# Attention turned on its side: keys on the partitions, no row maximum, strided heads in blocks of seven classes, gate logits computed transposed, and a flag that guards a second, shifted version

## The chip, the cores and the metric

The kernel runs on one core of one Trainium2 chip. The metric is the device time of one execution in microseconds (us), lower is better. The time before is the median of 8 executions. A profiled execution gives the trace that is read below; it is one more execution with its own time.

## What is computed

The program is attention followed by a mixture of experts with one expert per token. There are 8 batches (b), 8 heads of 64, and 576 positions. Heads 0 to 3 are *local*: position s sees keys s-31 to s. Heads 4 to 7 are *strided*: position s sees the earlier keys whose position has the same remainder modulo 32. Cut to what matters:

```python
scores = q @ k.T / 8
scores = where(mask_local or mask_strided, scores, -1e9)
scores = scores - max(scores)                  # per query row
attn = exp(scores); attn = attn / (sum(attn) + 1e-9)
x = attn @ v                                   # (8, 576, 512) after joining the heads
logits, local_gate = x @ w_gate, sigmoid(x @ w_local)
e = argmax(logits) if s == 0 or local_gate < 0.5 else the previous token's e
out = softmax(logits)[e] * (relu(x @ w1[e]) @ w2[e])   # w1: 512x1024, w2: 1024x512, 8 experts
```

Everything is float32.

## The kernel before, in words

Three stages follow one another.

**Attention** (`attention`, L82 to L309) works through 64 units in the order batch, pair of heads, half: `Unit(b, pair, g)`. Pairs 0 and 1 are local, 2 and 3 strided. Queries lie on the partitions. A local unit has three blocks of 96 queries against 128 keys, for two heads; a strided unit has four blocks of 72 queries against 72 keys. One unit goes through:

- `scores`: per head one matmul that writes the mask into PSUM (L175, bf16), then one matmul per block on top of it (L180, `sps`). The two heads of a pair sit on partitions 0 to 63 and 64 to 127. VectorE takes the row maximum (L184) and subtracts it (L187), ScalarE does the exponential (L189).
- `turn`: the exponentials are transposed block by block on TensorE (L197, `tps`), and ScalarE copies them to SBUF (L200).
- `values`: one matmul per block against v with a column of ones appended (L210). VectorE adds 1e-9 to the row sum, takes its reciprocal, and scales (L219 to L221).
- After a second pair, `store_x` writes 96 or 72 rows at a time to the DRAM tensor `xd` through SyncE's queue; `turn_x` transposes x into `xT` (L241, with ScalarE's copies L245 and L247).
- Once per batch `gates` computes the logits: 24 float32 matmuls with 96 columns of `xT` as the stationary operand and nine columns of the gate weights moving (L255).

A float32 matmul shows as two records in the profile, a transpose and a bf16 matmul as one. The order is that of a software pipeline (L284 to L309): step n does the scores of unit n, the transposes of n-1, the values of n-2, `turn_x` and `gates` of n-3; a planner may move instructions within it. Loads of the next batch's group are issued on SyncE when a group begins. During batch 1 the weights of expert 0 are loaded and GpSimd forms sums of their quarters (`Weights.ready`, L507 and L512).

**Routing** (`route`, L312 to L485) turns the gate results into tables of rows for each expert: small VectorE steps in a chain and the matmuls L475. A part for experts with over 6 tiles of 128 rows and their remainder is skipped by a branch unless it is needed.

**Experts** (`experts`, L526 on) gathers rows from `xd` with indirect DMAs, multiplies with a two-by-two scheme of seven products (L608 and L644, and L684 and L692 for a single tile), and scatters the result. The list after the last expert (the rows that didn't fit) is skipped by a branch on `count`.

Of the kernel before, what the change touches and what calls it, by code (L numbers as in the profile page):

```python
# [8 lines left out]
F32 = mybir.dt.float32  # L9
# [9 lines left out]
P = 128  # L19
# [17 lines left out]

QP = 3
XT = 2 * QP + 1
NT = E * XT  # L40
OT = 2 * (N // (2 * P) - QP)
# [30 lines left out]
@with_exitstack  # L72
def attention_then_scomoe(ctx: ExitStack, tc: tile.TileContext, q, k, vl, vs, wg, w1, w2, out):
    nc = tc.nc
    once = ctx.enter_context(tc.tile_pool(name="once", bufs=1))
    dram = ctx.enter_context(tc.tile_pool(name="dram", bufs=1, space=DRAM))
    xd = dram.tile([N, D], F32, name="xd")

    ident = once.tile([P, P], F32, name="ident")
    make_identity(nc, ident)  # L80
    gi = once.tile([P, NT + OT], I32, name="gi")
    si = once.tile([P, NT + OT], I32, name="si")  # L82
    gate = once.tile([P, NT + OT], F32, name="gate")
    pick = once.tile([1, E], I32, name="pick")
    oet = once.tile([1, OT], I32, name="oet")
    on = once.tile([1, 1], I32, name="on")
    tabs = gi, si, gate, pick, oet, on
    one = Weights(once)

    with ExitStack() as first:  # L90
        routing = first.enter_context(tc.tile_pool(name="routing", bufs=1))
        probs = routing.tile([LQ, LT, B, E], F32, name="probs")
        codes = routing.tile([LQ, LT, B, E], F32, name="codes")
        with ExitStack() as part:
            attention(part, tc, q, k, vl, vs, wg, xd, ident, probs, codes, lambda: one.ready(nc, w1, w2, 0))
        with ExitStack() as part:
            route(part, tc, ident, probs, codes, tabs)
    with ExitStack() as part:
        with tc.manual_schedule():
            experts(part, tc, xd, w1, w2, out, ident, tabs, one)  # L100


def attention(ctx, tc, q, k, vl, vs, wg, xd, ident, probs, codes, weights):
# [183 lines left out]
    for n in range(len(units) + 3):  # L287
        if n < len(units):
            u = units[n]
            if u.g == 0 and u.pair % 2 == 0:  # L290
                b, grp = u.b + 1, u.pair // 2
                if b < B:
                    load(b, grp)
                if b == 2 and grp == 1:
                    weights()
            scores(u)
# [15 lines left out]
def route(ctx, tc, ident, probs, codes, tabs):  # L312

    nc = tc.nc
    gi, si, gate, pick, oet, on = tabs
# [63 lines left out]
    nn = rp.tile([R, 2], F32, name="nn")  # L379
    nc.vector.tensor_copy(nn, nps[:, 0:2])  # L380
    qi = rp.tile([R, 1], I32, name="qi")
    nc.vector.tensor_scalar(qi, nn[:, 0:1], float(P - 1), None, Alu.add)
    nc.vector.tensor_scalar(qi, qi, 8, None, Alu.arith_shift_right)
    qf = rp.tile([R, 1], F32, name="qf")
    nc.vector.tensor_scalar(qf, qi, 1, None, Alu.max)
    ov = rp.tile([R, 1], F32, name="ov")
    nc.vector.tensor_scalar(ov, qf, -float(QP), 0.0, Alu.add, Alu.max)
    nc.tensor.matmul(nps[:, 2:3], lhsT=less[0:E, :], rhs=ov[0:E], start=True, stop=True)
    nc.tensor.matmul(nps[0:1, 3:4], lhsT=ones[0:E, 0:1], rhs=ov[0:E], start=True, stop=True)
    q2 = rp.tile([R, 1], F32, name="q2")  # L390
    nc.vector.tensor_scalar(q2, qf, float(2 * P), None, Alu.mult)
    pk = rp.tile([R, 1], F32, name="pk")
    nc.vector.tensor_scalar(pk, qf, float(QP), 2.0, Alu.min, Alu.mult)
    nc.vector.tensor_scalar(pk, pk, -2.0, None, Alu.add)
    nc.vector.scalar_tensor_tensor(pk, nn[:, 0:1], q2, pk, Alu.is_gt, Alu.add)
    pps = pp.tile([1, E + OT], F32, name="pps")
    nc.tensor.matmul(pps[:, 0:E], lhsT=pk[0:E], rhs=ident[0:E, 0:E], start=True, stop=True)
    nc.vector.tensor_copy(pick, pps[:, 0:E])
    nc.vector.tensor_copy(on, nps[0:1, 3:4])
    obase = rp.tile([R, 1], F32, name="obase")  # L400
    nc.vector.tensor_copy(obase, nps[:, 2:3])
    oend = rp.tile([E, 1], F32, name="oend")
    nc.vector.tensor_tensor(oend, obase[0:E], ov[0:E], op=Alu.add)
    past = rp.tile([E, OT], F32, name="past")
    nc.vector.tensor_scalar(past, io[0:E, 0:OT], 0.5, None, Alu.mult)
    pasti = rp.tile([E, OT], I32, name="pasti")
    nc.vector.tensor_scalar(past, past, -0.25, None, Alu.add)
    nc.vector.tensor_copy(pasti, past)
    nc.vector.tensor_copy(past, pasti)
    nc.vector.tensor_scalar(past, past, oend, None, Alu.is_ge)  # L410
    nc.tensor.matmul(pps[:, E:], lhsT=ones[0:E, 0:1], rhs=past, start=True, stop=True)
    nc.vector.tensor_scalar(oet, pps[:, E:], float(E - 1), None, Alu.min)

    first = rp.tile([R, 1], F32, name="first")
    nc.vector.tensor_scalar(first, er, float(XT * P), None, Alu.mult)

    far = rp.tile([R, 1], F32, name="far")
    nc.vector.tensor_scalar(far, obase, float(2 * P), float((E * XT - 2 * QP) * P), Alu.mult, Alu.add)
    nc.vector.tensor_tensor(far, far, first, op=Alu.subtract)
    isov = rp.tile([R, 1], F32, name="isov")  # L420
    nc.vector.tensor_scalar(isov, ov, 0.0, None, Alu.is_gt)
    nc.vector.tensor_tensor(far, far, isov, op=Alu.mult)
    rest = rp.tile([R, 1], F32, name="rest")
    nc.vector.tensor_scalar(rest, q2, -1.0, float(2 * QP * P), Alu.mult, Alu.add)
    nc.vector.tensor_tensor(rest, rest, far, op=Alu.subtract)
    rank0 = rp.tile([R, 1], F32, name="rank0")
    nc.vector.tensor_scalar(rank0, nn[:, 1:2], -1.0, None, Alu.add)
    rank = rp.tile([R, S], F32, name="rank")
    nc.vector.tensor_scalar(rank, cum, rank0, None, Alu.add)
    sa = rp.tile([R, S], F32, name="sa")  # L430
    nc.vector.tensor_scalar(sa, rank, float(2 * QP * P), far, Alu.is_ge, Alu.mult)
    sb = rp.tile([R, S], F32, name="sb")
    nc.vector.tensor_scalar(sb, rank, q2, rest, Alu.is_ge, Alu.mult)
    nc.vector.scalar_tensor_tensor(rank, rank, first, sa, Alu.add, Alu.add)
    nc.vector.tensor_tensor(rank, rank, sb, op=Alu.add)
    slot = rp.tile([R, S], F32, name="slot")
    nc.vector.tensor_tensor(slot, rank, hot, op=Alu.mult)
# [17 lines left out]

    lane = rp.tile([LQ, CM, P], F32, name="lane")
    for a, n in ((0, NT), (NT, OT)):
        if a:
            more = tc.If(nc.values_load(on[0:1, 0:1], engines=[ET.PE, ET.DVE, ET.Activation, ET.Pool], min_val=0,
                                        max_val=OT // 2,  # L460
                                        skip_runtime_bounds_check_because="a count of at most 15 pairs") > 0)
            more.__enter__()
        put = rp.tile([LQ, CM, 2, n], F32, name=f"put{a}")
        at = rp.tile([LQ, CM, n], F32, name=f"at{a}")
        nc.vector.tensor_tensor(at, across(io[0:LQ, a:a + n], [LQ, CM, n]), spread(hi, [LQ, CM, n]), op=Alu.is_equal)
        nc.gpsimd.tensor_tensor(put[:, :, 0], at, spread(tok, [LQ, CM, n]), op=Alu.mult)
        nc.vector.tensor_tensor(put[:, :, 1], at, spread(pt, [LQ, CM, n]), op=Alu.mult)
        tab = pp.tile([P, 2, n], F32, name=f"tab{a}")
        for t in range(LT):
            c = slice(t * B, (t + 1) * B)  # L470
            if not a:
                nc.vector.tensor_tensor(lane[:, c], across(io[0:LQ], [LQ, B, P]), spread(lo[:, c], [LQ, B, P]),
                                        op=Alu.is_equal)
            for i in range(t * B, (t + 1) * B):
                nc.tensor.matmul(tab, lhsT=lane[:, i], rhs=put[:, i], start=(i == 0), stop=(i == CM - 1))  # L475
        nc.scalar.copy(out=gate[:, a:a + n], in_=tab[:, 1])
        row = rp.tile([P, n], F32, name=f"rowf{a}")
        nc.vector.tensor_scalar(row, tab[:, 0], -1.0, 0.0, Alu.add, Alu.max)
        nc.vector.tensor_copy(gi[:, a:a + n], row)
        skip = rp.tile([P, n], F32, name=f"skip{a}")  # L480
        nc.vector.tensor_scalar(skip, tab[:, 0], 0.0, float(SKIP), Alu.is_equal, Alu.mult)
        nc.vector.tensor_tensor(row, row, skip, op=Alu.add)
        nc.vector.tensor_copy(si[:, a:a + n], row)
        if a:
            more.__exit__(None, None, None)  # L485
# [315 lines left out]
```

## Time and profile before

| | us |
|---|---|
| median of 8 executions (lowest, highest) | 1054.32 (1029.85, 1064.69) |
| the profiled execution | 1041.75 |
| its span, first to last instruction | 1040.0 |
| attention: first score matmul L180 to the last gate step on VectorE | 6.42 to 414.67 |
| routing: first matmul L358 to the first transpose of the experts L569 | 414.69 to 476.88 |
| experts: L569 to the end of the last scatter's issue | 476.88 to 1025.61 |
| busy over the span: TensorE matmul, weight load | 959.6, 863.3 |
| busy over the span: VectorE, ScalarE, GpSimd | 428.1, 240.2, 249.7 |

The parts of such a page: busy time of each engine, then the span in 40 slices (26 us each) with the clock granted to TensorE, then the DMA queues, then the chain of work that ended last, then the costliest groups. Groups are named by line, engine, operation and tile (`out<-in`), with the number of instructions, the busy time, and the mean duration of one. Matmuls overlap in the pipeline, so a price per matmul is read from start to start in the timeline, not from a mean duration.

### The profile page before, as it was taken

The numbers are of one execution on the slowest core, as the hardware profiler recorded it, in microseconds if no ns is written. First come the engines' busy times: TensorE is split into PE (matmuls) and PEld (weight loads), VectorE is DVE, ScalarE is ACT, GpSimd is POOL, SyncE is SP. The second block draws the span as 40 slices with busy tenths as digits, with TensorE's granted clock in tenths as the row PEclk, the third lists the DMA queues.
The fourth block names the chain that finished last, engine by engine and source line by source line (L and its number), as shares of the span: only waits on it lengthen the run. The fifth ranks groups of instructions, "written<-read, shape, count | busy, mean of one in ns | idle before, by whom it ended". The sixth has DMA issues, their size and how long they took to land.

```text
span 1040.0 us, 16153 instructions
## 1 busy us (share of the span) xinstructions
PE 959.6 (92%) x6632; PEld 863.3 (83%) x6632; DVE 428.1 (41%) x870; ACT 240.2 (23%) x389; POOL 249.7 (24%) x227
## 2 busy tenths in 40 slices
PE   7999999999999998286999898999999999899993
PEld 6888888888888888276998797979989989798893
DVE  6643434343444433831333535325333343532431
ACT  3422222222232321001222122222222222222220
POOL 1330000000000000204332625348173272533000
PEclk9855555555555555557999999999999999999997
DMA  9651414132322001006006043060520515201000
GB/s 320 231 201 50 144 47 135 59 109 86 101 93 67 27 5 42 1 1 244 22 21 209 34 149 105 21 214 22 190 77 21 197 43 177 76 21 41 29 21 19
DMA packets 35523, 95.54 MB, mean 92 GB/s; under 512 B 3278, under 2 KB 12494, under 8 KB 34768
## 3 DMA queue, kind: packets, MB, share of 16 engines
q1 hardware_dynamic: 28416, 73.58, 20.6%
q0 software_dynamic: 6400, 19.93, 5.7%
q8 instruction: 67, 1.10, 0.4%
q14 instruction: 112, 0.92, 0.3%
q10 hardware_dynamic: 528, 0.02, 0.0%
HBM read 74.64 MB, written 19.92 MB: 91 GB/s over the span
## 4 chain that ended last, share of the span: by engine, by line
PE 48%; issue 3%; DVE 3%; DMA 1%; ACT 0%; POOL 0%; ACTq 0%; DVEq 0%; POOLq 0%
PE lps L608 23%; PE mps L644 20%; PE xps L569 2%; PE lps L684 1%; PE mps L692 1%; DVE k L637 1%; PE tab L475 1%; DMA xfirst<-xd,gi 1%; DVE k L639 1%; DVE h L596 0%; DVE k L638 0%; ACT q L653 0%; POOL out_dram L583 0%; ACT xfirst L562 0%; ACT p L615 0%
## 5 line engine op out<-in xcount | busy, mean ns | idle before, releaser
L644 PE MATMUL mps<-wt,k 128*128 128x256 f32 x456 | 103.5, 384 | 6.9 <-DVE k L638 4.4
L180 PEld LDWEIGHTS sps<-kt,qt 64*72 64x72 f32 (+1 forms) x896 | 75.8, 232 | 33.5 <-issue 29.7
L583 POOL DMA_INDIRECT out_dram<-y,si x40 | 40.0, 1001 | 262.3 <-DVE y L596 241.5
L180 PE MATMUL sps<-kt,qt 64*72 64x72 f32 (+1 forms) x896 | 100.9, 365 | 2.1 <-DMA kt<-in_k_dram 2.1
L644 PEld LDWEIGHTS mps<-wt,k 128*128 128x128 f32 x456 | 86.2, 192 | 18.9 <-DVE k L638 4.9
L644 PE MATMUL mps<-w2t,h 128*128 128x256 f32 x304 | 76.8, 398 | 13.8 <-ACT q L653 9.0
L322 POOL IOTA rowi<- 64x1 int32 x1 | 0.1, 128 | 344.1 <-DVE gsm L281 344.1
L644 PEld LDWEIGHTS mps<-w2t,h 128*128 128x128 f32 x304 | 58.4, 199 | 24.0 <-ACT q L653 11.4
L184 DVE TENSOR_REDUCE mx<-sps 96x6 f32<-96x768 f32 (+1 forms) x64 | 54.6, 853 | 51.3 <-PE sps L180 51.2
L200 ACT COPY et<-tps 128x576 f32<-128x576 f32 (+1 forms) x64 | 40.8, 638 | 146.8 <-PE tps L197 146.8
L197 PE MATMUL tps<-ident,e 72*72 72x72 f32 (+1 forms) x448 | 71.6, 330 | 0.0
L596 DVE TENSOR_TENSOR h<-lps,u 128x512 f32<-128x512 f32 x57 | 39.4, 692 | 67.9 <-PE lps L608 58.7
L197 PEld LDWEIGHTS tps<-ident,e 72*72 72x72 f32 (+1 forms) x448 | 56.2, 184 | 12.5 <-issue 5.0
L210 PE MATMUL tps<-vst,et 72*72 72x65 f32 x512 | 64.5, 313 | 0.8 <-DVE xs L221 0.7
L595 ACT ACTIVATE h<-h 128x512 f32<-128x512 f32 x57 | 35.9, 630 | 118.9 <-DVE h L596 109.1
L210 PEld LDWEIGHTS tps<-vst,et 72*72 72x72 f32 x512 | 61.4, 227 | 2.3 <-PE tps L197 0.6
L210 PE MATMUL tps<-vlt,et 128*96 128x65 f32 x384 | 63.3, 346 | 0.0
L255 PEld LDWEIGHTS tps<-wgs,xT 128*96 128x96 f32 x384 | 60.7, 273 | 2.9 <-ACT xT L247 2.9
L608 PE MATMUL lps<-ttmore,ws 128*128 128x128 f32 x528 | 62.6, 275 | 0.0
L255 PE MATMUL tps<-wgs,xT 128*96 128x9 f32 x384 | 61.4, 304 | 1.0 <-ACT xT L247 1.0
L210 PEld LDWEIGHTS tps<-vlt,et 128*96 128x96 f32 x384 | 59.9, 260 | 1.8
L608 PEld LDWEIGHTS lps<-ttmore,ws 128*128 128x128 f32 x528 | 60.7, 192 | 0.0
(212 smaller groups left out, 1540.6 us busy)
## 6 DMA issues: line engine op xcount, KB each, us to landing
w1t<-in_w_dram SPq DMA_DIRECT2D x8, 2048.0 KB, 9.0
w2t<-in_w_dram SPq DMA_DIRECT2D x8, 2048.0 KB
kt<-in_k_dram SPq DMA_DIRECT2D x16, 608.0 KB, 4.9
qt<-in_q_dram SPq DMA_DIRECT2D x16, 576.0 KB, 3.7
vlt<-in_vl_dram SPq DMA_DIRECT2D x8, 780.0 KB, 11.9
vst<-in_vs_dram SPq DMA_DIRECT2D x8, 585.0 KB
xd<-xl SPq DMA_DIRECT2D x8, 576.0 KB, 3.9
xd<-xs SPq DMA_DIRECT2D x8, 576.0 KB
```

Of the source, the lines that this page charges most:

```text
L180: nc.tensor.matmul(ps[0:w, h, i * kb:(i + 1) * kb], lhsT=qt[r, i2, c:c + w], rhs=kt[r, i2, c:c + kb], start=False, stop=(i == m - 1))
L184: nc.vector.tensor_reduce(mx[0:w, :, 0:m], sv, axis=AX.X, op=Alu.max)
L197: nc.tensor.transpose(ps[0:kb, h, i * w:(i + 1) * w], u.e[0:w, h, i * kb:(i + 1) * kb], ident[0:w, 0:w])
L200: nc.scalar.copy(out=et[0:kb], in_=ps[0:kb, :, 0:288])
L210: nc.tensor.matmul(ps[0:w, h, i * V1:(i + 1) * V1], lhsT=u.et[0:kb, h, i * w:(i + 1) * w], rhs=vt[0:kb, 2 * i2 + h, u.g * m + i, :], start ...
L255: nc.tensor.matmul(ps[0:LQ, 0, t * (E + 1):(t + 1) * (E + 1)], lhsT=xT[:, kk, t * LQ:(t + 1) * LQ], rhs=wgs[:, kk, :], start=(kk == 0), st ...
L569: nc.tensor.transpose(ps[:, kk], r.x[:, i, kk * P:(kk + 1) * P], ident)
L583: s = nc.gpsimd.indirect_dma_start(out=out, out_offset=bass.IndirectOffsetOnAxis(ap=si[:, j:j + 1], axis=0), in_=y[:, i], in_offset=None, ...
L595: relu = lambda o, i: nc.scalar.activation(o, i, Act.Relu)
L596: add = lambda o, i, p: nc.vector.tensor_tensor(o, p, i, op=Alu.add)
L608: nc.tensor.matmul(ps[:, f], lhsT=m[:, kk, f * P:(f + 1) * P], rhs=v[:, kk], start=(start and f == 0 and kk == 0), stop=(kk == 1), skip_gr ...
L644: nc.tensor.matmul(ps[:, 0:256], lhsT=m[:, f], rhs=v[:, f], start=(start and f == 0), stop=(f == 3), skip_group_check=True)
```

## The change

- **Scores** are computed turned: the keys are the stationary operand and lie on the partitions of the result, the queries move. So the exponentials come out in the form that `values` needs, and `turn` with its copy is gone.
- **No maximum** is taken. ScalarE takes the exponential straight from PSUM. A local unit has no mask matmuls any more: VectorE multiplies the exponentials with a 0/1 mask in SBUF (`mask`, L239). A strided unit still has two bf16 mask matmuls.
- **Strided heads** are laid out by remainder: 18 positions of one remainder follow one another, and a block is seven remainders, 126 queries against 126 keys. The 576 positions make four blocks of 126 and one of 72; a unit with g = 0 has two blocks of 126, one with g = 1 has two of 126 and one of 72.
- The 1e-9 isn't added; the reciprocal row sums are kept for all units in `sums`.
- **The gate logits** are computed transposed: 32 columns (nine used) of the gate weights are stationary and 288 positions move, one matmul for each of the four quarters of the model dimension and each half of the positions, into four strips of 32 partitions (L307, `logits`). A second small matmul per 96 positions adds up the four strips and turns the result (L319, `gates`).
- q and k of a pair come in one DMA; pairs are loaded four ahead. `store_x` is issued on GpSimd's queue: one DMA for a local pair of pairs, five for a strided one. The attention is put under the same manual order as the experts: step n does scores and mask of unit n, values and scaling of n-2, `turn_x` of n-4, `logits` of n-5, `gates` of n-6.
- **The flag**: `route` checks that every reciprocal sum lies between 1e-12 and 1e12 and that no expert has more rows than its tables hold. The tables for the rows that didn't fit and the list after the last expert are gone. After the experts, a branch on the flag runs `general`: the whole program once more in a form with the row maximum (`shifted_attention` is the old attention), routing by tiles and plain expert products.

```diff
-            attention(part, tc, q, k, vl, vs, wg, xd, ident, probs, codes, lambda: one.ready(nc, w1, w2, 0))
+                with tc.manual_schedule():
+                    attention(part, tc, qkl, qks, vl, vs, wg, xd, ident, probs, codes, sums,
+                              lambda: one.ready(nc, w1, w2, 0))
...
+    redo = nc.values_load(flag, min_val=0, max_val=P + N, ...)
+    with tc.If(redo > 0):
+        with ExitStack() as slow:
+            general(slow, tc, q, k, vl2, vs2, wg2, w1, w2, xd, out, ident)
...
+    inp = ctx.enter_context(tc.tile_pool(name="inp", bufs=6))
+    vals = ctx.enter_context(tc.tile_pool(name="vals", bufs=2))
+    work = ctx.enter_context(tc.tile_pool(name="work", bufs=4))
...
     def scores(u):
...
+        if not u.local:
+            for h in range(2):
+                nc.tensor.matmul(ps[0:GK, h, 0:n], lhsT=identb[0:GK, 0:GK],
+                                 rhs=maskS.rearrange("p a x -> p (a x)")[:, 0:n], start=True, stop=False, ...)
+        for j, w, c in sp:
+            keys = S + j * LQ if u.local else S + j * GK
+            m = kb if u.local else w
             for h in range(2):
                 r = slice(h * DH, (h + 1) * DH)
-                nc.tensor.matmul(ps[0:w, h, i * kb:(i + 1) * kb], lhsT=qt[r, i2, c:c + w],
-                                 rhs=kt[r, i2, c:c + kb], start=False, stop=(i == m - 1))
-        nc.vector.tensor_reduce(mx[0:w, :, 0:m], sv, axis=AX.X, op=Alu.max)
-        nc.vector.tensor_tensor(ev.rearrange("p h (i x) -> p h i x", x=kb), sv,
-                                spread(mx[0:w, :, 0:m], [w, 2, m, kb]), op=Alu.subtract)
-        nc.scalar.activation(ev, ev, Act.Exp, bias=0.0, scale=1.0 / DH ** 0.5)
+                at = j * (LQ if u.local else GK)
+                nc.tensor.matmul(ps[0:m, h, c:c + w], lhsT=t[r, keys:keys + m], rhs=t[r, at:at + w], ...)
+        nc.scalar.activation(e[0:kb, :, 0:n], ps[0:kb, :, 0:n], Act.Exp, bias=0.0, scale=1.0 / DH ** 0.5)
-    def turn(u):
...
+    def mask(u):
+        if u.local:
...
+            nc.vector.tensor_tensor(ev, ev, m..., op=Alu.mult)
     def values(u):
...
+                nc.tensor.matmul(ps[0:w, h, i], lhsT=u.e[0:m, h, c:c + w], rhs=vt[0:m, j, 2 * i2 + h], ...)
+    def store_x(u):
+        if u.local:
+            nc.gpsimd.dma_start(out=dst.rearrange("(t p) d -> p t d", p=LQ), in_=src[0:LQ])
+        else:
+            for j in range(GT):
+                nc.gpsimd.dma_start(out=dst[j * GC:j * GC + w // PL], in_=src[0:w, j])
...
+    def logits(b):
+        for a in range(2):
+            for kk in range(DK):
+                nc.tensor.matmul(ps[32 * kk:32 * kk + 32, a, 0:S // 2], lhsT=wgs[:, kk],
+                                 rhs=xT[:, kk, a * (S // 2):(a + 1) * (S // 2)], start=True, stop=True, ...)
+        nc.scalar.copy(out=lT[0:64]..., in_=ps[0:64, :, 0:S // 2])
+        nc.scalar.copy(out=lT[64:]..., in_=ps[64:, :, 0:S // 2]...)
     def gates(b):
-        for t in range(LT):
-            for kk in range(DK):
-                nc.tensor.matmul(ps[0:LQ, 0, t * (E + 1):(t + 1) * (E + 1)],
-                                 lhsT=xT[:, kk, t * LQ:(t + 1) * LQ], rhs=wgs[:, kk, :], ...)
+        for t in range(LT):
+            nc.tensor.matmul(lt[:, t], lhsT=st["lT", b][:, t * LQ:(t + 1) * LQ], rhs=fold, ...)
...
+    for n in range(len(units) + 7):
+        if n < len(units):
+            if n % 2 == 0 and n // 2 + ahead < len(order):
+                load(*order[n // 2 + ahead])
+            if n == 12:
+                weights()
+            scores(units[n])
+            mask(units[n])
+        if 0 <= n - 2 < len(units):
+            values(u)
+            norm(u)
+            if u.g == 1 and u.pair % 2 == 1:
+                store_x(u)
+        if 0 <= n - 4 < len(units) and units[n - 4].g == 1:
+            turn_x(units[n - 4].b, units[n - 4].pair)
+        for d, do in ((5, logits), (6, gates)):
...
```

## The prediction

> **What bounds the kernel now.** I read the page's 40 slices first:
>
> ```profile
> PE   7999999999999998286999898999999999899993
> PEclk9855555555555555557999999999999999999997
> ```
>
> TensorE is full nearly everywhere, and the clock granted to it is half from the third slice to the end of the routing, full in the experts. So the attention (to 414.7 us) is a TensorE stage at half clock. The view of stretches has one batch in each 52 us, with VectorE at 22.34, ScalarE at 14.50 and DMA at 0.30: nothing else is near its limit.
>
> ```profile
> 208.00:260.00 52.00, 52.00 (x364) 45.08 (x364) 22.34 (x53) 14.50 (x21) 0.00 (x0) 0.50 0.30 97
> ```
>
> (Columns: stretch, length, busy PE, PEld, DVE, ACT, POOL with counts, clock, DMA share, GB/s.) Then the timeline of TensorE, at half clock and in the early stretch at full clock. Columns: start, duration, what; a price is start to start.
>
> ```profile
> 138.84 0.84 PE L175 MATMUL sps<-maskL,identb 96*96 96x384 bf16 x2
> 139.62 1.60 PE L180 MATMUL sps<-kt,qt 64*96 64x128 f32 x12
> 141.15 1.22 PE L197 MATMUL tps<-ident,e 96*128 96x96 f32 x6
> 142.16 2.07 PE L210 MATMUL tps<-vlt,et 128*96 128x65 f32 x12
> ...
> 146.86 7.85 PE L255 MATMUL tps<-wgs,xT 128*96 128x9 f32 x48
> 154.64 1.17 PE L180 MATMUL sps<-kt,qt 64*96 64x128 f32 x6
> ```
>
> ```profile
> 36.20 0.49 PE L175 MATMUL sps<-maskL,identb 96*96 96x384 bf16 x2
> 36.62 0.90 PE L180 MATMUL sps<-kt,qt 64*96 64x128 f32 x12
> 37.45 0.71 PE L197 MATMUL tps<-ident,e 96*128 96x96 f32 x6
> 38.01 1.16 PE L210 MATMUL tps<-vlt,et 128*96 128x65 f32 x12
> 39.00 0.33 PE L175 MATMUL sps<-maskL,identb 96*96 96x384 bf16 x1
> ```
>
> A local unit takes 5.2 us at half clock (0.78 + 1.53 + 1.01 + 1.87) and 2.8 at full (0.42 + 0.83 + 0.56 + 0.99). A strided one takes 4.86 at half (0.61 + 1.38 + 0.96 + 1.91). A batch at half clock is 4 x 5.2 + 4 x 4.86 + four turns of x at 0.96 + the gates at 7.78 = 51.9, the period seen. The twelve score matmuls started at 8.75 took 1.53 to the next, like those at half clock: the kernel also starts slow, whatever the clock column says there, and speeds up at about 12.
>
> Why does the clock fall? It falls in the first burst of gate matmuls:
>
> ```profile
> 40.00:44.00 4.00, 3.47 (x33) 3.26 (x34) 0.84 (x4) 1.71 (x2) 2.18 (x2) 0.85 0.52 162
> 44.00:60.00 16.00, 16.00 (x110) 13.79 (x112) 7.70 (x25) 3.40 (x6) 0.00 (x0) 0.50 0.58 208
> ```
>
> These stream 9 columns per load of 96. After that it never rises in 350 us of full TensorE. So "busy" isn't what raises it. My inference is that the clock follows how much of the array streams. At half clock a moving column costs 1.67 ns (16 records of 128 columns on all rows from 478.88 to 482.30). By that price, rows weighted, an old local unit fills 74%, a strided one 56%; the table matmuls L475 (96 of 128 rows, 12 us without a rise) 75%; the start (masks and scores alone, rise) 75 to 78%; the experts' L608 (rise at 483) 100%. The level that raises it is then just over 75%. At full clock the old strided units filled 44% for many windows without a fall, the gate burst under 25% made it fall.
>
> The Trainium skill ("TensorE: Matmul & The Clock Gate", Part 1) has the clock rise after some 3.4 us of sustained activity and fall after an idle window; here 350 us of busy TensorE stayed at 0.50, so the measurement decides. By the page the new attention would be at full clock from about 9 us on, and the sum below would be 20 us lower.
>
> **The change, part by part (per batch).** Prices at full / half clock.
>
> *Scores, local*: 12 records as before, 96 columns instead of 128 and 128 weight columns instead of 96: priced at the old 0.069 / 0.128 each (0.83 / 1.53). The two mask matmuls go.
> *Values, local*: unchanged, 0.99 / 1.87.
> Four local units: 7.3 / 13.6.
> *Strided*: mask pairs 0.33 and 0.40 / 0.55 and 0.66 (by columns from 0.61 at 288). Scores of 126: 8 records at 0.069 / 0.128; of 72: 4 at 0.042 / 0.086. Values cost by weight columns (72: 0.064 / 0.12; 96: 0.083 / 0.156), so 126 is 0.107 / 0.20. The two-block unit: 1.74 / 3.2, the three-block unit 2.23 / 4.1. Two of each: 7.9 / 14.6.
> *The transposes `turn`* go: 8 x about 1 us at half clock.
> *Turns of x*: 2.1 / 3.9.
> *Gates*: 12 records of 96 weight columns, 1.0 / 1.9, against 48 (7.78).
> *Logits*: 16 records of 288 columns. No row shows matmuls into strips of 32 partitions. One after another they cost 0.243 each (from 256 columns at 0.216 in L644), 3.9 / 7.7; if the four strips run side by side, as the two heads' score records partly do (0.069 against 0.112 for 128 columns on all rows), 1.0 / 2. I take the middle.
> The skill's same page (Part 3, column tiles) has three strips give 2.38 times; by that the logits cost some 1.5 / 3 and the sum falls by about 7 us.
> Sum: 19.3 to 22.2 at full clock, I take 20.5; 36 to 42 at half, I take 38; against 52.
>
> *Beside TensorE.* ScalarE: eight exponentials at 0.62 to 0.74 (from 0.68 for 576 elements), 2.9 of xT copies, about 1.9 for the two logit copies: 10.5. VectorE loses maxima and subtractions and gains four masks at 0.69: about 11. Both under 20.5. Values come two steps after the scores, so exponential plus mask (1.4) has 3.6 us. DMA: 5.05 MB per batch; at the 330 GB/s of the stretch 12 to 40 that is 15 us, hidden with a margin of 5. SyncE issues six DMAs per batch instead of eight. GpSimd's queue gets six stores; a 128-row indirect one shows 1.0, so 6 to 10 us per batch on an engine that was at 0.00. Only one thing is queued there: at step 12 the weight sums (16 at 1.25 = 20 us, and the wait for 4 MB, about 10) stand ahead of the store of batch 1's local half, whose tile is needed again at step 26, some 32 us later. It just fits; if not, up to 10 us once.
>
> *The mask reads two SBUF tiles*, and so do the weight sums. Such a VectorE instruction can stand still beside them:
>
> ```profile
> 575.54 6.21 DVE L637 TENSOR_TENSOR k<-h,h 128x512 f32<-128x512 f32 x1 [2.51 <-issue]
> 581.79 0.69 DVE L638 TENSOR_TENSOR k<-k,h 128x512 f32<-128x512 f32 x1
> ```
>
> (GpSimd was in such sums from 571.36 to 581.2.) The 20 us of sums meet about four masks, each 0 to 5.5 us late, behind which `norm` queues and for which `values` waits; TensorE has 2 us of slack per step. Bounds 0 and 16; I take 8, with a share for a fall of the clock.
>
> *Routing*: about 13 VectorE steps of 0.14 to 0.2 go (`past`, `far`, `oet`), the check of the sums comes (two passes over 384 elements and a maximum-like reduction, 0.5 each by `sel` and `pt`). Between -1 and +2, taken as 0. *The end*: a load of the flag and a jump in place of those of `count`; the chain shows 2.6 to 3.5 us for a jump of a switch. Between -1 and +5, taken as 0 since one replaces the other.
>
> **The sum.** Scores start at 5 (one 606 KB load instead of two). The clock is low at first: new local units fill 65%, strided scores with masks up to 76%, the logits 85 to 100%. So it rises between about 20 and, at the latest, the first logits, step 12, 5 + 1.5 x 34 = 56. I take 45: 40 us do 1.2 batches. The other 6.8 at 20.5 are 139, to 184; the tail of six steps 7; the sums beside the masks 8. Routing starts at about 199 instead of 414.7: 216 us less than the profiled execution's 1041.75 is 826. That execution lies 12.6 below the median, with a spread of 35; I forecast **832**, own range 800 to 860.
>
> **The rivals.**
> *A: as summed.* For it: at full clock the new units fill 62%, more than the old ones that held it; only `gates` is thin, 1 us per batch, with 46% in its window. Against: any stall of some 3 us. **0.52.**
> *B: the clock alternates*, falling at `gates` or a stall in each batch and coming back with the next logits. Half the time cold is 29 per batch: 5 + 8 x 29 + 8 = 245, a gain of 170: 872 (850 to 915). **0.22.**
> *C: it stays at half throughout*, since the new matmuls fill less of the array than the old and the strips may not count. 5 + 8 x 38 + 8 = 317, a gain of 98: 944 (925 to 976). For it: the old attention never came back. **0.20.**
> *D: slower, by the flag.* If any reciprocal sum is outside 1e-12 to 1e12, or one expert has more than 6 x 128 + 128 rows, the whole is done again: the old attention 405, routing 60, experts over 550, about 1850 in all. Against: q and k are 0.1 times a normal, so sums lie between 1 and 32; and the trace has 40 scatters, 19 pairs and two singles, with none from the list after the last expert. **0.03.**
> The rest, **0.03**, is another bound at full clock (DMA at 15 of 20.5), ending near 900.
>
> The range: 800 to 950 leaves out D, the upper part of C and the bottom tail of A. Faster by over 2%: 0.95; within 2%, about what a measurement of this kernel can tell: 0.02; slower: 0.03.
>
> **What would show it.** `tps` transposes of `e` and the L184 and L187 groups are gone; the clock row reads high in slices from about 50 us to the routing (A), mixed (B) or 5 (C); sixteen logit records take 1 to 4 us at full clock; L239 means well over 0.7 only while GpSimd sums weights; experts as before, some 549 us. The prediction is wrong if the clock follows something else than the array's fill, or if the strips, the masks or the queue of stores stall TensorE.

## The result, and the profile after

| | before | after |
|---|---|---|
| median (lowest, highest), us | 1046.23 (1029.85, 1069.19) | 840.37 (815.72, 849.03) |
| profiled execution, its span | 1041.75, 1040.0 | 817.68, 815.9 |
| attention: first score to routing | 6.42 to 414.69 | 4.91 to 183.44 |
| routing: to the first transpose of the experts | 62.19 | 62.00 |
| experts: from there to the end of the span | 563.1 | 570.5 |
| TensorE busy over the span | 959.6 | 727.8 |

The ratio of the times is **0.788**, 95% interval 0.7828 to 0.7931; it goes by the executions near the fastest of each kernel (for the changed one three, at 815.7 to 819.3), which is why it is lower than the ratio of the two medians, 0.803. The forecast was 832 with a range of 800 to 950.

The same two rows of the 40 slices (20.4 us each now):

```profile
PE   7999999973459999899699999879999998999991
PEclk9999999995558999999999999989999999999996
```

Half clock is left in three slices, the routing. Before, it filled sixteen. One warning: the clock column reads full until the first recorded change of the clock, so the start is read from the prices. The timeline of TensorE (start, duration, what) around that first change:

```profile
20.18 1.46 PE L229 MATMUL sps<-qk 64*126 64x126 f32 x12
21.57 1.23 PE L250 MATMUL vps<-vl,e 128*96 128x65 f32 x12
22.64 0.67 PE L289 MATMUL tps<-ident,xl 96*128 96x96 f32 x6
...
25.39 0.83 PE L229 MATMUL sps<-qk 64*126 64x126 f32 x12
```

The twelve score records of a strided unit take 1.39 from start to start at 20.18 and 0.77 later (the same line at 108.11): the clock doubles at about 22 us, in the first strided units. From there to the routing a batch takes 20.66 us, logits to logits (101.01, 121.67, 142.33). The stretch of one batch (columns as in the prediction):

```profile
110.00:131.00 21.00, 21.00 (x242) 18.31 (x241) 10.79 (x37) 9.91 (x17) 3.86 (x6) 1.00 0.79 262
```

TensorE is still the bound, now at full clock, with VectorE at half its time and the DMA at 0.79. The new pieces of a batch:

```profile
101.01 1.18 PE L307 MATMUL tps<-xT,wgs 128*32 128x288 f32 x16
102.12 0.49 PE L220 MATMUL sps<-maskS,identb 126*126 126x324 bf16 x2
...
104.87 1.11 PE L319 MATMUL vps<-fold,lT 128*96 128x9 f32 x12
105.84 0.41 PE L220 MATMUL sps<-maskS,identb 126*126 126x252 bf16 x2
```

The sixteen logit records take 1.11, the twelve of the gates 0.97. Against 7.78 for the old gates at half clock, this is 2.1.

### The profile page after: what moved, and what is told of

Read it like the earlier page. It is cut to its first block, busy times and chain, and to the rows that moved or that the text cites. A ratio compares the mean times of both kernels' runs of the same rounds, so it can differ in the third digit from the quotient of the medians.

```text
span 815.9 us, 13775 instructions
## 1 busy us (share of the span) xinstructions
PE 727.8 (89%) x5526; PEld 660.4 (81%) x5526; DVE 345.2 (42%) x725; ACT 203.2 (25%) x357; POOL 285.6 (35%) x277
## 4 chain that ended last, share of the span: by engine, by line
PE 83%; DVE 6%; issue 5%; DMA 2%; ACT 1%; ACTq 0%; POOL 0%; DVEq 0%; SPq 0%; POOLq 0%
PE lps L651 28%; PE mps L687 25%; PE vps L250 9%; PE sps L229 6%; PE tab L520 3%; PE xps L612 2%; DVE k L680 2%; PE lps L727 2%; PE mps L735 2%; PE sps L220 1%; PE tps L307 1%; PE tps L294 1%; PE tps L289 1%; PE vps L319 1%; DVE put L513 1%
## 5 line engine op out<-in xcount | busy, mean ns | idle before, releaser
L229 PE MATMUL sps<-qk 64*128 64x96 f32 (+2 forms) x704 | 57.4, 297 | 5.8 <-DMA qk<-in_qkl_dram 5.8
L229 PEld LDWEIGHTS sps<-qk 64*128 64x128 f32 (+2 forms) x704 | 46.6, 195 | 15.5 <-issue 6.7
L232 ACT ACTIVATE e<-sps 128x576 f32<-128x576 f32 (+1 forms) x64 | 41.7, 651 | 51.9 <-PE sps L229 51.8
L555 POOL TENSOR_TENSOR ws<-w1t 128x512 f32<-128x512 f32 x32 | 43.4, 1373 | 11.2 <-DMA w1t<-in_w_dram 10.1
L651 PE MATMUL lps<-ttfirst,ws 128*128 128x128 f32 x384 | 45.5, 275 | 0.0
L651 PEld LDWEIGHTS lps<-ttfirst,ws 128*128 128x128 f32 x384 | 44.2, 192 | 0.0
L279 POOL DMA_DIRECT2D xd<-xs x40 | 24.8, 626 | 53.5 <-DVE xs L267 44.0
L651 PE MATMUL lps<-xtmore,w1t 128*128 128x128 f32 x352 | 42.9, 275 | 0.0
L651 PEld LDWEIGHTS lps<-xtmore,w1t 128*128 128x128 f32 x352 | 41.9, 192 | 0.6
L250 PE MATMUL vps<-vl,e 128*96 128x65 f32 x384 | 42.3, 263 | 0.0
L555 POOL TENSOR_TENSOR wt<-w2t 128x512 f32<-128x512 f32 x32 | 41.0, 1308 | 0.0
```

Source lines behind the costliest of these rows:

```text
L229: nc.tensor.matmul(ps[0:m, h, c:c + w], lhsT=t[r, keys:keys + m], rhs=t[r, at:at + w], start=(u.local and c == 0), stop=True, skip_group_c ...
L232: nc.scalar.activation(e[0:kb, :, 0:n], ps[0:kb, :, 0:n], Act.Exp, bias=0.0, scale=1.0 / DH ** 0.5)
L250: nc.tensor.matmul(ps[0:w, h, i], lhsT=u.e[0:m, h, c:c + w], rhs=vt[0:m, j, 2 * i2 + h], start=(i == 0 and h == 0), stop=True, skip_group_ ...
L279: nc.gpsimd.dma_start(out=dst[j * GC:j * GC + w // PL], in_=src[0:w, j])
L555: return lambda: nc.gpsimd.tensor_tensor(o[:, c], x[:, c], y[:, c], op=op)
L651: nc.tensor.matmul(ps[:, f], lhsT=m[:, kk, f * P:(f + 1) * P], rhs=v[:, kk], start=(start and f == 0 and kk == 0), stop=(kk == 1), skip_gr ...
```

## The experiments

My theory was the one on record: the clock follows how much of the array streams, the old gates' thin matmuls pull it down, and dense matmuls bring it up. The rivals were that it follows something else (the mere number of matmuls, gaps, the new units), and that the gain is in the work that was removed.

### Only the gates turned

The kernel before, with the logits and gates alone changed; nothing is left out.

```diff
-            nc.tensor.matmul(ps[0:LQ, 0, ...9 columns of t], lhsT=xT[:, kk, ...96 of t], rhs=wgs[:, kk, :], ...)
+            nc.tensor.matmul(ps[32 * kk:32 * kk + 32, a, 0:S // 2], lhsT=wgs[:, kk], rhs=xT[:, kk, ...288 of a], ...)
...
+            nc.tensor.matmul(ps[0:LQ, 0, ...9 columns of t], lhsT=lT[:, ...96 of t], rhs=fold, ...)
```

> The kernel before with one part of the change alone: the gate logits are computed transposed (16 records of 288 columns and 12 of 9 instead of 48 of 9 columns), all else old. Theory, the thin burst of gate matmuls is what made the clock fall: the attention stays at full clock after its start, a batch takes 4 x 2.8 + 4 x 2.6 + 4 x 0.55 + 2.1 = 26 us instead of 52, the attention ends near 225 instead of 414.7, and the run takes about 850 (835 to 880). Rival, the old units cannot hold full clock for long whatever the gates do: half clock nearly throughout, a gain of 8 x 4 to 6 us only, about 1000 to 1010.

Measured: 878.38 (877.41 to 902.24), ratio 0.8437 (0.8379 to 0.8496). The stretch at 198 us of its profile, of an execution that took 902.24:

```profile
198.00:224.00 26.00, 25.29 (x322) 21.15 (x322) 19.55 (x52) 14.51 (x21) 0.00 (x0) 1.00 0.40 127
```

The same transposes, maxima and scores as before, which ran 350 us at half clock, now run at 1.00 until the last gates. So by the two ratios about three quarters of the gain come with 7.8 us of gate work per batch replaced. The turned gates do two things here: the thin stretch at which the clock fell is gone, and dense records stand in its place. In this profile the clock records show the rise at 65.8, just as the first logits end (63.66 to 65.74), and full clock from there to 253.6. How much each of the two is worth was not separated. The time lies 28 above what I expected; this is taken up further down.

### Work added: a burst after the old gates

The kernel before, with five useless float32 matmuls of 512 columns after the gates of each batch. Work is added and none is left out. Four forms: on all 128 rows, on 96 rows, on 64 rows, and on 128 rows with only 32 weight columns. ROWS stands for 128, 96 or 64.

```diff
+            nc.tensor.matmul(ps[:, 0], lhsT=xT[0:ROWS, 0, 0:P], rhs=xT[0:ROWS, 1, 0:512], start=True, stop=True)
```

```diff
+            nc.tensor.matmul(ps[0:32, 0], lhsT=xT[:, 0, 0:32], rhs=xT[:, 1, 0:512], start=True, stop=True)
```

> The kernel before with five matmuls of 512 columns added after the gates of each batch (useless work, all 128 rows, 8.5 us at half clock, 4.3 at full). Theory, the clock is raised by filled rows and then held by the old units: it comes back in each burst and falls at the next gates, a batch takes about 36 us, about 930 (900 to 960), faster although work is added. Rival, the old units cannot hold it or nothing in the attention raises it: 8 x 5 to 8.5 us more, 1080 to 1115.

> As the run with the burst of all rows, but the five matmuls use 96 of the 128 rows: the same instructions and durations, 75% fill. Theory, the level lies just over 75% of the rows: the clock does not rise, 8 x 8.5 us more, about 1110. Rival, sustained streaming raises it whatever the rows: the same time as with 128 rows, about 930.

> The kernel before with the burst of five matmuls of 512 columns after the gates, on 64 of the 128 rows. Theory, revised after 96 rows did raise the clock: rows count, and the level lies between the 65% of the table matmuls (96 in 20.8 us, so the rows are idle in part) and 75%: at 50% the clock does not rise, 8 x 8.5 us more than before, about 1110. Rival, long streaming raises it whatever the rows: about 946, as with 128 and 96 rows.

> The same burst on all 128 rows with only 32 weight columns, as in one strip of the new logits. Theory, rows of the moving operand count and not the columns of weights: the clock rises, about 946. Rival, the share of the whole array counts (25% here): it does not rise, about 1110.

| burst | median, us | ratio (interval) |
|---|---|---|
| 128 rows | 946.03 | 0.9091 (0.8999 to 0.9182) |
| 96 rows | 948.95 | 0.9119 (0.9027 to 0.921) |
| 64 rows | 1094.98 | 1.0603 (1.0511 to 1.0696) |
| 128 rows, 32 weight columns | 961.54 | 0.9311 (0.9223 to 0.94) |

The stretch from 100 to 300 us, first with 128 rows, then 96, then 64, then 32 weight columns:

```profile
100.00:300.00 200.00, 194.07 (x2058) 156.06 (x2055) 121.82 (x282) 79.28 (x114) 0.00 (x0) 0.91 0.36 111
```

```profile
100.00:300.00 200.00, 195.25 (x2048) 153.15 (x2044) 121.65 (x282) 78.21 (x113) 0.00 (x0) 0.90 0.35 111
```

```profile
100.00:300.00 200.00, 200.00 (x1214) 159.71 (x1212) 71.48 (x172) 44.79 (x66) 0.00 (x0) 0.50 0.24 76
```

```profile
100.00:300.00 200.00, 196.81 (x1990) 147.81 (x1989) 118.47 (x283) 74.39 (x108) 0.00 (x0) 0.90 0.36 114
```

All the bursts keep TensorE busy for 6 to 9 us (with 64 rows the planner put six score records among the last ones). With 64 rows the clock stays at 0.50 in this stretch, and the kernel is 6% slower for them; with 128 rows it is 9% faster although it does more. 32 weight columns do as well as 128; the rows that stream make the difference. With 128 rows the clock alternates: in the trace's clock records it is full for 30.7 us and half for 6.8 in most batches, since the next gates pull it down again and the burst brings it back.

The 96-row burst was a miss: I had put the level "just over 75%". It came from the table matmuls, which I had taken for 75% filled; 96 of them take 20.8 us, 0.217 each, while 112 columns at 1.67 ns stream in 0.187, so they fill 0.75 x 0.187 / 0.217 = 65%. If rows times streaming time is the right measure, the level lies between 65 and 75%. The old local units, which the prediction put at 74%, never raised the clock in 350 us of the kernel before; with the 64-row burst one of them did so once, for a single 3.4 us at 340.6. So the level would be near the upper end.

### Everything but the turned gates

The changed kernel with the old nine-column gates (and the copies that put xT in order for them). Nothing is left out.

```diff
-                nc.tensor.matmul(ps[32 * kk:32 * kk + 32, a, 0:S // 2], lhsT=wgs[:, kk], rhs=xT[:, kk, ...288 of a], ...)
...
+                nc.tensor.matmul(lt[:, t], lhsT=xT[:, kk, ...96 of t], rhs=wgs[:, kk, 0:E + 1], ...)
```

> The changed kernel with the old form of the gates alone (48 records of 9 columns per batch; the copies after the turns of x put the strided positions back in order). Theory: the clock falls in each burst and comes back within some 10 us in the strided units, which fill up to 76%: 4.5 us more matmul time per batch and 3 to 5 lost at half clock, 860 to 890 against the 816 to 840 of the changed kernel. Rival, the new units hold the clock even over the burst: 2 us more per batch, about 833 to 855.

Measured: 961.04 (953.59 to 964.02), ratio 0.9212 (0.9123 to 0.9301). Both were wrong: it is 71 us above the top of what the theory gave. TensorE about the gates of one batch, and then the stretch of a batch and a half after:

```profile
133.56 1.22 PE L229 MATMUL sps<-qk 64*126 64x126 f32 x8
134.71 1.39 PE L250 MATMUL vps<-vl,e 128*96 128x65 f32 x12
135.93 5.53 PE L309 MATMUL tps<-wgs,xT 128*96 128x9 f32 x48
141.31 0.78 PE L220 MATMUL sps<-maskS,identb 126*126 126x324 bf16 x2
142.02 1.46 PE L229 MATMUL sps<-qk 64*126 64x126 f32 x12
```

```profile
190.00:230.00 40.00, 40.00 (x248) 36.83 (x246) 10.56 (x34) 9.01 (x15) 3.86 (x6) 0.50 0.38 113
```

By its prices the kernel runs at half clock from the start to 135.1. Then the clock records show full clock for 3.4 us, in a strided unit, but the gates that follow at once (48 records in 5.38, partly at full clock) lose it again; the mean over 150 to 310 us is 0.53. I had expected the new units to bring the clock up by themselves. They do so only now and then. It is the forecast's case C (half throughout), which was worth 944 there.

With the first experiment this makes a table of two by two (medians, with the ratios to the kernel before):

| | old units | new units |
|---|---|---|
| old gates | 1046 | 961 (ratio 0.9212) |
| turned gates | 878 (0.8437) | 840 (0.788) |

### A burst where the clock is low

Useless matmuls in the changed kernel: twelve of 128 columns at the start, while the first load is awaited; four of 512 before the table matmuls; eight of 512 while the first rows are gathered. Two small copies on ScalarE fill the operand of the four. Then the first twelve alone, in the changed kernel and in the kernel before with turned gates. Work is added, none is left out.

```diff
+    for i in range(12):
+        nc.tensor.matmul(warm[:, i % 2, 0:P], lhsT=ident, rhs=ident, start=True, stop=True)
...
+            for i in range(4):
+                nc.tensor.matmul(wps, lhsT=ident, rhs=warm, start=True, stop=True)
...
+    for i in range(8):
+        nc.tensor.matmul(wps..., lhsT=one.w1[:, 0, 0:P], rhs=one.w1[:, 1, 0:512], start=True, stop=True)
```

> The changed kernel with useless matmuls put where TensorE waits: 12 of 128 columns while the first load is awaited, 4 of 512 columns before the table matmuls of the routing, 8 of 512 during the first gathers. Theory: the clock rises by 9 us instead of 22 to 56, the table matmuls take 11 us instead of 21, the first expert starts at full clock: 7 + 10 + 3 us under the fast runs of the changed kernel, about 797, and the runs scatter less, since the first rise no longer hangs on a narrow margin. Rival, products with the identity do not count as fill, or the clock falls again in the waits: 815 to 845.

> The changed kernel with the 12 matmuls at the start alone. Theory, the changed kernel's runs of 815 and of 845 differ by when the clock first rises (22 us in the profile; if missed, only the first logits at about 56 raise it): all runs near 808 to 815. Rival, the scatter comes from the experts: a median near 830 with the same spread of 30.

> The kernel before with the turned gate logits and the 12 matmuls at the start: the old units at full clock throughout. Theory: 4 x 2.8 + 4 x 2.6 + 4 x 0.55 + 2.1 = 26 us per batch, the attention ends near 222, the run takes about 850 (840 to 865); so the clock is worth some 190 us and the fewer matmuls, at full clock, the 40 to 813. Rival, another bound holds the old units at full clock (VectorE has 21 of 26 us per batch): 865 to 885, as without the start.

| | median (lowest, highest), us | ratio (interval) |
|---|---|---|
| all three bursts | 798.33 (796.18, 801.92) | 0.7724 (0.7668 to 0.778) |
| start burst alone | 813.11 (809.85, 815.98) | 0.7863 (0.7808 to 0.7919) |
| old units, turned gates, start burst | 885.4 (883.57, 887.38) | 0.8546 (0.8482 to 0.8611) |

The first two came as expected, and the version with all three is faster than both kernels of this case. The group of table matmuls, in the changed kernel and with the bursts:

```profile
L520 PE MATMUL tab<-put,lane 96*128 96x112 f32 x96 | 20.8, 422 | 12.4 <-DVE put L513 12.4
```

```profile
L532 PE MATMUL tab<-put,lane 96*128 96x112 f32 x96 | 10.9, 276 | 0.5 <-DVE put L518 0.5
```

The third came as its rival had it, above what the theory gave, for two reasons that the trace shows. First, TensorE in the old units and the turned gates, with the start burst, around 50 us (the wait and its releaser in brackets):

```profile
48.98 0.73 PE L186 MATMUL sps<-kt,qt 64*72 64x72 f32 x14
53.04 0.64 PE L181 MATMUL sps<-maskS,identb 72*72 72x288 bf16 x2 [3.33 <-DVE e L193]
53.61 0.51 PE L186 MATMUL sps<-kt,qt 64*72 64x72 f32 x2
54.05 1.18 PE L203 MATMUL tps<-ident,e 72*72 72x72 f32 x8
```

and VectorE just before, in the same profile:

```profile
46.17 1.31 DVE L280 TENSOR_TENSOR ex<-lt,gmx 96x48 f32<-96x48 f32 x1
47.41 1.30 DVE L284 TENSOR_TENSOR eq<-lt,gmx 96x48 f32<-96x48 f32 x1
48.63 1.26 DVE L290 SCALAR_TENSOR_TENSOR fr<-lt,start 96x6 f32<-96x6 f32 x1
...
53.73 0.20 DVE L297 TENSOR_TENSOR probs<-ex,gsm 96x48 f32<-96x48 f32 x1
```

GpSimd forms the weight sums from 43.69 to 53.5. Gate steps of 0.2 take 1.3 there, TensorE waits 3.33, the clock falls and is half for the 37 us to 89. Second, a batch at full clock takes 28.3 us (logits at 115.89, 144.20, 172.51), not the 26 that I had counted with: 7 batches at 2.3 are 16. The fall costs about half of 37 and the wait, some 21 as an estimate; 850 and 16 and 21 make 887, against 885 measured. TensorE is busy for 27.54 of the 28.31 us of such a batch and VectorE for 22.0, so the missing part is no other engine that became the bound, but a wrong period and a fall of the clock. The period also accounts for most of the 28 by which the first experiment was off (8 x 2.3 = 18). One thing more: 885 is no better than the 878 without the start burst. In the old units the early rise bought nothing: here the gate steps met the sums, while in the first experiment's profile they did not.

### The same kernel again, and without the second version

The changed kernel unchanged, to see what its scatter is; and one in which the flag's branch and `general` are left out (the flag is still computed).

```diff
-    redo = nc.values_load(flag, min_val=0, max_val=P + N, ...)
-    with tc.If(redo > 0):
-        with ExitStack() as slow:
-            general(slow, tc, q, k, vl2, vs2, wg2, w1, w2, xd, out, ident)
```

> The changed kernel itself once more, beside the others on the same chip. Theory, its times hang on when the clock first rises: some near 816 (rise in the first strided units), some near 840 (rise at the first logits), a spread of 20 to 30 that the kernel with the matmuls at the start does not have (6). Rival, the scatter of the chip: all runs within 8.

> The changed kernel without the branch on the flag and the second version behind it (the check of the sums stays). Theory, the jump over the second version costs what the old jump over the list did: within 4 us of the changed kernel, a median in its range of 815 to 849. Rival, a load of the flag and a jump over a large block cost more at the end: 5 to 15 us less.

Measured, side by side on one chip: 829.75 (818.07 to 835.25) for the kernel again, 829.61 (810.75 to 831.04) without the branch. With a scatter of 17 and 20 us these times can't price the branch. The two profiles can (spans of 829.8 and 828.4 us). The last scatter, first with the branch, then without:

```profile
813.07 0.98 POOL L626 DMA_INDIRECT out_dram<-y,si  x1 [0.91 <-issue]
```

```profile
817.76 0.98 POOL L619 DMA_INDIRECT out_dram<-y,si  x1 [0.91 <-issue]
```

From its end to the end of the span there are 15.7 us with the branch (in the first profile of the changed kernel too) and 9.7 without. So the branch costs 6 us at the end, as the rival had it; the last scatter comes 4.7 us later in this profile, which hides most of them. The kernel before, with its branch on `count`, has 14.4.

The kernel's own scatter is 17 us there, somewhat under the 20 to 30 that I had expected. Its profile shows where most of it comes from:

```profile
50.25 1.06 PE L229 MATMUL sps<-qk 64*126 64x126 f32 x8
51.23 1.23 PE L250 MATMUL vps<-vl,e 128*96 128x65 f32 x12
...
62.05 0.91 PE L229 MATMUL sps<-qk 64*128 64x96 f32 x12
64.79 1.94 PE L250 MATMUL vps<-vs,e 126*126 126x65 f32 x8 [1.84 <-DVE sums L266]
66.66 1.60 PE L229 MATMUL sps<-qk 64*128 64x96 f32 x12
```

Here the first strided units (16 to 32 us) don't raise the clock; it comes up at about 51, just before the first logits (in the kernel without the branch at about 56, just after them). And at 64.79 TensorE waits 1.84 for VectorE, beside GpSimd's sums, and twelve scores take 1.53 again until about 82, when the clock comes back beside the second logits. The routing starts at 206.46 instead of 183.44. With the start burst, which fixes the first rise, the scatter is 6 us. So the time of the first rise makes most of the scatter, as far as four executions of each can tell; the experts take back 9 of the 23 us here. No profile is kept of an execution at the median of 840 or above, so what those lose beyond the 830 stays open.

### The weight sums broken up

The version with all three bursts; the sixteen sums of expert 0's weights are issued one to a step in steps 17 to 32, not in one train at step 12. Nothing is left out.

```diff
             if n == 12:
-                weights()
+                one.load(nc, w1, w2, 0)
+                todo = one.sums(nc)
+            if n > 16 and todo:
+                todo.pop(0)()
```

> The kernel with all useless bursts, whose sixteen sums of expert 0's weights on GpSimd are no longer issued in one go at step 12: the weights are loaded there, and one sum of about 1.25 us is issued in each of the steps 17 to 32 (a step takes some 2.56 us). Nothing is left out. In the runs that had full clock before these sums, TensorE waited 1.3 to 3.3 us for VectorE inside the sums (44 to 66 us), and the clock was half for the 20 to 37 us after that. Theory: it is the length of the unbroken train of sums that lets VectorE fall so far behind that TensorE stands still and loses its clock; broken up, VectorE catches up in between. Then TensorE has no wait for VectorE of over 1 us before the routing, the clock column reads 1.00 from the start to the last gates, and the time is 20/2 + 1.5 = 11 to 12 us below 798: 787 (783 to 792). Rival: the fall comes with any of these waits or from something else at that point (the thin matmuls of the gates); then the clock falls in batch 1 or 2 as before and the time is 795 to 802. Second rival: sums spread over sixteen steps meet more masks and gate steps, and TensorE loses more than now: over 803.

Measured: 798.1 (795.24 to 803.52), ratio 0.7696 (0.7659 to 0.7732): no gain over 798.33, as the first rival had it. GpSimd, VectorE and TensorE in its timeline:

```profile
58.52 0.78 POOL L279 DMA_DIRECT2D xd<-xl  x1 [3.72 <-DVE xl L272]
59.31 1.28 POOL L570 TENSOR_TENSOR ws<-w1t 128x512 f32<-128x512 f32 x1
60.54 2.49 POOL L570 TENSOR_TENSOR ws<-w1t,ws 128x512 f32<-128x512 f32 x2
63.00 1.26 POOL L570 TENSOR_TENSOR wt<-w2t 128x512 f32<-128x512 f32 x1
```

```profile
59.48 4.84 DVE L338 TENSOR_TENSOR eq<-eq,down 96x48 f32<-96x48 f32 x1
64.36 0.20 DVE L340 TENSOR_REDUCE code<-eq 96x6 f32<-96x48 f32 x1
```

```profile
66.46 1.58 PE L255 MATMUL vps<-vs,e 126*126 126x65 f32 x8 [2.02 <-DVE sums L271]
```

The sums weren't apart after all: the store of x stands ahead of them in GpSimd's queue and waits for `norm`, and when it is through, four sums follow at once. One VectorE step of 0.2 stands still for all four of them, 4.84 us, TensorE waits 2.02, and the clock is half for 20.5 us as before. So this doesn't settle whether it takes a long train; it shows that a train of 5 us is enough. Whether sums that really are single would keep the clock wasn't tried.

The Trainium skill ("SBUF — State Buffer", section "SBUF: two separate sides") has GpSimd and a VectorE instruction with two SBUF inputs share one pair of ports, which the one that starts first holds for its whole instruction. The 4.84 agrees with such a lock, but the wait lasted four GpSimd instructions, not the rest of one.

## Why the prediction was right, and where it was off

The prediction held: faster, 840 in a range of 800 to 950, 8 from the forecast, by the mechanism of case A. That it came so near is in part luck: the rise put at 45 and the 8 for the sums each stood between two outcomes, and in the batch the logits were priced too high and the values too low. By its own steps, against the profile with the early rise and the one with the late rise:

| step | forecast | early rise | late rise |
|---|---|---|---|
| first scores | 5 | 4.91 | 4.85 |
| the clock rises | 45 (20 to 56) | 22 | 51 |
| a batch at full clock | 20.5 | 20.66 | 20.66 |
| masks beside the weight sums | 8 (0 to 16) | 0 | 1.84 waited, 17 us at half clock: 10 |
| routing starts | 199 | 183.44 | 206.46 |
| routing, against 62.19 before | 0 | -0.2 | -0.1 |
| experts to the end, against 563.1 | 0 | +7.4 | -1.8 |
| span | 824 | 815.9 | 829.8 |

- **The clock.** Right that the old thin gates lose it and that rows streaming raise it: turned gates alone, the bursts of 64 and 128 rows. Wrong in the level, "just over 75%", because the table matmuls were priced as full streams; they fill 65%, and 75% was enough. And wrong in "at full clock the new units fill 62%, more than the old ones that held it" as a sign that the new units matter for the clock: the old units hold it just as well once the gates are turned (1.00 from 66 us to 250).
- **When it rises.** "Between about 20 and, at the latest, the first logits" was right at both ends: 22 in one profile, 51 and 56 in others. Strided units are at the edge of raising it; with the old gates in place they hardly ever do.
- **Batch sum.** The prices were right in sum, as errors cancelled. The strips run fully side by side: 1.11 for the logits against the middle of 2.5, at the lower bound. The values of 126 columns cost 0.93 to 1.02 for eight where 0.86 was forecast, those of 96 columns 1.07 to 1.16 for twelve where 0.99 was. GpSimd's stores cost 3.86 us per batch (0.62 and 0.77 each) against 6 to 10; no wait for them shows on TensorE.
- **Masks and sums.** The masks were the wrong victims. They took 1.13 to 1.71 beside the sums in the early-rise profile, and TensorE was busy throughout:

```profile
50.30 1.55 DVE L239 TENSOR_TENSOR e<-e,maskL 128x576 f32<-128x576 f32 x1
52.32 1.28 DVE L239 TENSOR_TENSOR e<-e,maskL 128x576 f32<-128x576 f32 x1
54.86 1.71 DVE L239 TENSOR_TENSOR e<-e,maskL 128x576 f32<-128x576 f32 x1 [0.31 <-ACT e L232]
57.19 1.13 DVE L239 TENSOR_TENSOR e<-e,maskL 128x576 f32<-128x576 f32 x1
```

  What stalls TensorE is the chain of small gate steps, when enough of it falls into the sums. In the early-rise profile only its end did (three steps of 1.0 to 1.2), and TensorE did not wait; in the late one all from 58.00 to 64.02, and it waited. Which of the two happens depends on when the clock rose. The 8 stood between the two outcomes, 0 and 10.
- **Routing** was right at 0. **The experts** vary by 9 us between the two profiles with the same code: TensorE waited 36 us in all in the one and 29 in the other, 10.4 of it for the first gather in both, the rest mostly for ScalarE's `q` and VectorE's `k`; after such a wait the clock records show it at half for 3.4 or 6.8 us. This wasn't in the forecast.
- **The flag (D)**: no second pass ran. Its branch costs 6 us, and the time from the last scatter to the end went from 14.4 to 15.7 us; the 0 for one branch in place of another was off by 1.4, inside its range.
- **Case B** did not occur in the two profiles of the changed kernel, but is what the bursts of 128 rows do to the kernel before; **case C** is the new units with the old gates.

## What to carry to other kernels

Where TensorE is always busy and yet slow, read the granted clock by stage, and look for the stretch that streams few columns per weight load: turning one thin product, nine columns wide, so that 288 columns move was worth 168 us here, twice the 85 that all of the rest was worth with the old gates in place. Where such a product can't be turned, a burst of dense matmuls on all rows, even useless ones, can pay for itself at the start, after a wait or after the thin stretch; it need not, as 885 against 878 showed. And before moving work to an idle GpSimd, look for the small VectorE steps beside it, and for what stands ahead of it in its queue.

## What the runs showed of the hardware that was not expected

- In these runs the clock is raised by rows that stream, not by busy time or by weight columns: bursts on 96 and 128 rows raise it, on 64 rows they don't, and 32 of 128 weight columns suffice. The Trainium skill ("TensorE: Matmul & The Clock Gate", Part 1) has it rise after a window of some 3.4 us of sustained activity. The length agrees, since the times between two changes in the clock records are whole multiples of 3.41 us (30.7, 6.8, 17.07, 61.4); that activity is enough does not: 200 us of TensorE at 200.00 busy stayed at 0.50 with the 64-row burst.
- A thin stretch shorter than 8 us costs far more than itself: the old gates in the new kernel last 5.4 to 7.8 us per batch, and with them it is 121 us slower; their own longer time is at most 8 x 5.7 = 46 of these, the rest goes with the clock that they lose.
- Four strips of 32 partitions run side by side in float32: 16 records of 288 columns in 1.11 us, 0.069 each, where 0.243 for one after another was the estimate from 0.216 for 256 columns.
- One VectorE step of 0.2 us stood still for 4.84 us through four GpSimd instructions in a row.
